# Transposing the normalized attention output: TensorE and a DVE copy, or the DMA crossbar

## The chip, the core and the metric

The kernel runs on one core of a Trainium2 chip. The metric is device time in microseconds for one execution. The core's engines that matter here are TensorE (PE in the profile, its weight loads PEld), VectorE (DVE), ScalarE (ACT), GpSimd (POOL, which here issues the loads) and SyncE (SP, which here does nothing but issue DMAs). Each engine works through its own instructions in order, and semaphores hold an instruction back until what it needs is there.

## The reference: attention with a relative bias, then a mixture of adapters

The first half is attention over 8 batches, 8 heads, 576 positions and a head size of 64, with a bias that depends on the distance of two positions; the second half adds to each of the 4608 tokens a gated sum of the two best of 8 low-rank adapters.

```python
scores = scale * np.matmul(q, k.transpose(0, 1, 3, 2)) + bias
attn = exp(scores - max) ; attn = attn / sum(attn)
x = np.matmul(attn, v)            # then rows = tokens (4608), columns = 8 heads x 64 = 512
logits = x @ w_gate               # 512 -> 8
topk = the two largest; w = softmax over those two
out = x + sum_k w_k * ((x @ A[e_k]) @ B[e_k])     # A: 512 -> 16, B: 16 -> 512
```

The products `x @ w_gate` and `x @ A` sum over the 512 columns of x. TensorE sums over partitions, and attention leaves x with tokens on the partitions. So x has to be transposed between the two halves. That transpose is what the change is about.

## The kernel before, in words

The outer loop (L502) runs over 32 pairs of heads, four per batch, and one more turn, `i` = 32, that finishes the last pair. In turn `i`, five blocks `g` of 128 keys (the fifth holds the 64 tail keys of both heads) each get score matmuls (`qk`, L258 to L268), an exponential on ACT (L275) and a multiplication by the bias factor on DVE (`band`, L282 to L293). In the same turn PE also transposes k and q of the next pair (`transposes`, L247, copied out by DVE in L250) and multiplies the probabilities of the previous pair with v (`pv_main`, L304 and L310, at g = 1; `pv_rest`, L324 to L336, at g = 2). DVE divides those products by their sums and writes them into x as bf16 (`norm_main`, L347 and L348, token blocks 0 to 2; `norm_rest`, L356 to L360, block 3 and the 64 tail tokens).

When the last pair of a batch has been normalized (turn `i` a multiple of 4, g = 2), the second half for that batch is put in a queue of pieces (`pieces`, L477). At g = 0, 3 and 4 of each turn one piece is taken from it (L528, L529). The pieces are, in order: `m_x` half 0, `m_x` half 1, for odd batches `m_xtail` (the 128 tail tokens of two batches, by a selecting matmul), `m_gate` (logits, top two, weights; the matmul is L399, its copy out L404), the same for the tail, `m_z` (L431, L436), `m_zT` (L447, L449), four `m_out` (matmul L455, sum L457, store issued by SP in L460) and for odd batches `m_outt` (L465 to L475, two stores). What is left after the last turn is run in a row.

Odd batches have 14 pieces and a batch has 12 places, so two pieces are left over for the next batch: batches 2, 4 and 6 begin with the last `m_out` and the `m_outt` of the batch before. Seen from the place where x is complete (turn `i`, g = 2), the first matmul of the gate is therefore issued in turn `i`+1 at g = 0 for batch 0, at g = 3 for batches 1, 3 and 5, at g = 4 for batches 2, 4 and 6, and for batch 7 in the closing row, directly after `m_xtail`.

`m_x` works on half of a batch's 512 main tokens: eight transposes of 128x128 on PE into a PSUM tile `xps` (L375), and one DVE copy of 128x1024 into `xT` (L377). `xps` comes from the pool `acc`, which has two buffers for everything but the scores: the transposed k and q, the attention products, and all tiles of the second half. `xT` has two buffers as well.

Loads are issued by POOL, which also converts f32 to bf16 on the way; the loads of v for the batch after next and its tails are held back until `pv_rest` of the last pair has freed their buffer, that is, until about the time when x is complete (L69, L96, L105). There is no planner: the order on each engine is the order of the calls.

Of the kernel before, what the change touches and what calls it, by code (L numbers as in the profile page):

```python
# [11 lines left out]
BF16 = mybir.dt.bfloat16  # L12
# [15 lines left out]
def kernel(  # L28
# [11 lines left out]
    nc = tc.nc  # L40
# [22 lines left out]
    acp = ctx.enter_context(tc.tile_pool(name="acc_ps", bufs=2, space=PSUM))  # L63
# [49 lines left out]
    ident = cp.tile([128, 128], BF16, tag="ident")  # L113
# [40 lines left out]
    for h0, h1 in ((0, 2), (2, H)):  # L154
        nc.sync.dma_start(
            out=Mr[:, h0:h1, :],
            in_=bass.AP(tensor=gt.tensor, offset=gt.offset + h0 * 512,
                        ap=[[1, 128], [512, h1 - h0], [1, MW]]))
        if h0 == 0:
            for e in range(2):  # L160
                nc.sync.dma_start(
                    out=MHr[e * 64:(e + 1) * 64],
                    in_=bass.AP(tensor=gt.tensor, offset=gt.offset + e * 512 + 192,
                                ap=[[1, 64], [1024, HP], [1, 192]]))
# [54 lines left out]
    for i in range(2):  # L219
        t = cp.tile([128, HP, 3, 128], BF16, name=f"tlT{i}", tag=f"tlT{i}")  # L220
# [74 lines left out]
    def pv_main(i):  # L295
        b, hp = divmod(i, HP)
        vn, vt = vns[b % 2], vts[b % 2]
        acc = acp.tile([128, 3, 2, D1], FP32, name="pvA", tag="acc")
        first = True
        for g in range(5):  # L300
            p = probs[(i, g)]
            for qb in range(3):
                if g == 4:
                    nc.tensor.matmul(acc[:, qb], lhsT=p[:, qb * 128:(qb + 1) * 128],  # L304
                                     rhs=vt[:, hp, :], start=False, stop=True,
                                     skip_group_check=True)
                    continue
                for h in range(2):
                    o = h * 512 + qb * 128
                    nc.tensor.matmul(acc[:, qb, h, :], lhsT=p[:, o:o + 128],  # L310
                                     rhs=vn[:, g, 2 * hp + h, :], start=first,
                                     stop=False, skip_group_check=True)
                    first = False
        return acc

    def pv_rest(i):
        b, hp = divmod(i, HP)
        vn, vt = vns[b % 2], vts[b % 2]
        acc = acp.tile([128, 2, 2, D1], FP32, name="pvB", tag="acc")
        first = True  # L320
        for g in range(5):
            p = probs[(i, g)]
            if g == 4:
                nc.tensor.matmul(acc[:, 0], lhsT=p[:, 384:512],  # L324
                                 rhs=vt[:, hp, :], start=False, stop=True,
                                 skip_group_check=True)
                nc.tensor.matmul(acc[:, 1], lhsT=p[:, 512:640], rhs=vt[:, hp, :],
                                 start=False, stop=True, skip_group_check=True)
                continue
            for h in range(2):  # L330
                o = h * 512 + 384
                nc.tensor.matmul(acc[:, 0, h, :], lhsT=p[:, o:o + 128],
                                 rhs=vn[:, g, 2 * hp + h, :], start=first,
                                 stop=False, skip_group_check=True)
                first = False
            nc.tensor.matmul(acc[:, 1], lhsT=p[:, 1024:1152],  # L336
                             rhs=vn[:, g, 2 * hp:2 * hp + 2, :], start=False,
                             stop=False, skip_group_check=True)
        return acc
# [27 lines left out]
    def m_x(b, half):  # L367
        x = xs[b]
        if half == 0:
            st[(b, "xT")] = xp.tile([128, 4, S4], BF16, name="xT", tag="xT")  # L370
        xT = st[(b, "xT")]
        ps = acp.tile([128, 4, 256], BF16, name="xps", tag="acc")
        for t2 in range(2):
            for c in range(4):
                nc.tensor.transpose(ps[:, c, t2 * 128:(t2 + 1) * 128],  # L375
                                    x[:, 2 * half + t2, 2 * c:2 * c + 2, :], ident)
        nc.vector.tensor_copy(xT[:, :, half * 256:(half + 1) * 256], ps)  # L377

    def m_xtail(b):

# [96 lines left out]
    def pieces(b):  # L477
        km, kt = (b, "m"), (b, "t")
        l = [lambda: m_x(b, 0), lambda: m_x(b, 1)]
        tl = b % 2 == 1  # L480
        if tl:
            l.append(lambda: m_xtail(b))
        l.append(lambda: m_gate(km, st[(b, "xT")], 4))
        if tl:
            l.append(lambda: m_gate(kt, st[(b, "xT", "t")], 1))
        l.append(lambda: m_z(km, st[(b, "xT")], 4))
        if tl:
            l.append(lambda: m_z(kt, st[(b, "xT", "t")], 1))
        l.append(lambda: m_zT(km, 4))
        if tl:  # L490
            l.append(lambda: m_zT(kt, 1))
        for t in range(4):
            l.append(lambda t=t: m_out(b, t))
        if tl:
            l.append(lambda: m_outt(b))
        return l
# [5 lines left out]
    for i in range(NPAIR + 1):  # L502
# [10 lines left out]
        for g in range(5):  # L513
# [6 lines left out]
            if g == 1 and i > 0:  # L520
                acc = pv_main(i - 1)
                norm_main(i - 1, acc)
            if g == 2 and i > 0:
                acc = pv_rest(i - 1)
# [41 lines left out]
```

The softmax here doesn't subtract the row's maximum and nothing guards it: scores larger than these inputs give would overflow.

## Time and profile before

| what | value |
|---|---|
| time, median of two runs | 258.7 us (258.33 and 259.07) |
| span of the profiled execution, first to last instruction | 257.7 us |
| own time of the profiled execution | not given apart; the two runs stand 0.6 and 1.4 us above the span, 1.0 by their median |
| DVE busy | 205.9 us, 641 instructions |
| PE busy | 189.7 us, 2576 matmuls |
| ACT busy | 165.4 us, 174 instructions |
| L375, transposes of x on PE | 128, 9.8 us in all |
| L377, copies of them on DVE | 16, 10.9 us in all, 682 ns each |
| L399, gate matmuls | 128 for the main tokens, 166 ns each |
| loads, queue of POOL | 14.16 MB, 112768 packets, 89.6% of the time of 16 DMA engines |
| DMAs of SP and others, hardware queue | 10.97 MB, 14.6% |

Busy times of different engines overlap, and so do the packets of different DMA queues, so the shares do not add up to one. The batches follow each other at about 26 to 27 us; the last pair is normalized near 241 us, and the rest is the closing row for batch 7.

### The profile page before, as it was taken

Reading aid. Unit: us, or ns where it says so; the run is one execution under the profiler, and the core shown is the slowest. Engines: PE = TensorE matmul, PEld = TensorE weight load, DVE = VectorE, ACT = ScalarE, POOL = GpSimd, SP = SyncE. Lnnn points to the kernel's source line nnn. Section 1 sums busy time; section 2 is a strip of 40 time slices with the busy share of each in tenths; the row PEclk is TensorE's granted clock in tenths of the full one; section 3 lists DMA queues with packets and bytes.
Section 4 is the critical chain, followed back from the end, with each engine's and each line's share of the span. In section 5 each row is a group of like instructions: output and inputs, shape, how many; then the busy total and the mean of one; then the engine's idle time right before and its main releaser. Section 6 shows DMA issues by size and latency. Waiting matters only on the chain.

```text
span 257.7 us, 6522 instructions
## 1 busy us (share of the span) xinstructions
PE 189.7 (74%) x2576; PEld 120.1 (47%) x2576; DVE 205.9 (80%) x641; ACT 165.4 (64%) x174; POOL 117.3 (46%) x155
## 2 busy tenths in 40 slices
PE   0020698797878868897799778987898788888852
PEld 0010255465545655456356554564465544664710
DVE  3200678999898888999979898989998889989972
ACT  2000469897769767886688677867796678868100
POOL 8997999745733591185508560549052000000000
PEclk9999999999999999999889999999999999999965
DMA  4999999969893999399939992799969003202205
GB/s 27 141 154 153 94 131 114 137 42 99 85 201 54 105 84 84 122 146 85 163 95 107 58 142 34 133 166 101 147 109 69 0 3 123 84 3 83 85 21 183
DMA packets 124759, 25.56 MB, mean 99 GB/s; under 512 B 118960, under 2 KB 119992, under 8 KB 124728
## 3 DMA queue, kind: packets, MB, share of 16 engines
q0 software_dynamic: 112768, 14.16, 89.6%
q1 hardware_dynamic: 11960, 10.97, 14.6%
q8 instruction: 20, 0.33, 0.5%
q14 instruction: 11, 0.09, 0.1%
HBM read 29.84 MB, written 9.45 MB: 152 GB/s over the span
## 4 chain that ended last, share of the span: by engine, by line
DVE 50%; PE 26%; ACT 7%; POOL 6%; issue 5%; DMA 3%; ACTq 0%; POOLq 0%; DVEq 0%
PE pvA L310 11%; DVE x L348 6%; PE sc L262 5%; DVE x L360 3%; DVE kqT L250 3%; DMA vn_86<-in_v_dram 3%; DVE o L457 3%; DVE xT L377 3%; PE pvA L304 2%; PE kqps L247 2%; DVE rcA L347 2%; POOL qn L69 2%; DVE rmB L358 2%; PE sc L258 1%; PE dl L455 1%
## 5 line engine op out<-in xcount | busy, mean ns | idle before, releaser
L262 PE MATMUL sc<-kqT 64*128 64x512 bf16 x256 | 51.8, 402 | 0.0
L69 POOL DMA_DIRECT2D kn<-in_k_dram x36 | 31.2, 896 | 19.1 <-PE kqps L247 18.2
L69 POOL DMA_DIRECT2D qn<-in_q_dram x36 | 31.0, 906 | 1.6 <-DMA vn_86<-in_v_dram 1.5
L258 PE MATMUL sc<-tlT_184,kqT 128*128 128x128 bf16 x64 | 14.5, 226 | 18.3 <-DVE kqT L250 13.0
L69 POOL DMA_DIRECT2D vn_87<-in_v_dram x16 | 14.0, 894 | 28.4 <-PE pvB L336 28.4
L69 POOL DMA_DIRECT2D vn_86<-in_v_dram x16 | 14.0, 896 | 27.7 <-PE pvB L336 27.6
L262 PEld LDWEIGHTS <-kqT 64*128 64x128 bf16 x256 | 12.4, 93 | 26.5 <-issue 17.4
L250 DVE COPY kqT<-kqps 128x1024 bf16<-128x1024 bf16 x32 | 21.8, 683 | 3.5 <-PE kqps L247 3.4
L457 DVE TENSOR_TENSOR o<-dl,x 128x512 f32<-128x512 f32 x32 | 21.8, 683 | 1.6 <-DMA out_dram<-o 0.8
L258 PEld LDWEIGHTS <-kqT 128*128 128x128 bf16 x128 | 12.8, 100 | 17.7 <-DVE kqT L250 13.2
L348 DVE TENSOR_TENSOR x<-pvA,rcA 128x384 bf16<-128x384 f32 x32 | 17.8, 557 | 1.1
L455 PE MATMUL dl<-Bb,zT 128*128 128x512 bf16 x32 | 13.3, 421 | 6.8 <-DVE zT L449 2.8
L275 ACT ACTIVATE p_227<-sc 128x1152 bf16<-128x1152 f32 x1 | 1.1, 1131 | 23.4 <-PE sc L262 23.4
L239 DVE COPY tlT_184<-tps 64x512 bf16<-64x512 bf16 x8 | 3.4, 419 | 15.4 <-POOL tlT_184 L221 15.3
L258 PE MATMUL sc<-tlT_186,kqT 128*128 128x128 bf16 x64 | 14.2, 222 | 1.7 <-ACT p_571 L275 0.7
L360 DVE TENSOR_TENSOR x<-pvB,rmB 128x256 bf16<-128x256 f32 x32 | 13.6, 424 | 1.1
L347 DVE RECIPROCAL rcA<-pvA 128x6 f32<-128x6 f32 x32 | 6.2, 195 | 10.1 <-PE pvA L304 9.9
L247 PE MATMUL kqps<-ident,kn 128*128 128x128 bf16 x128 | 13.3, 229 | 1.0 <-DVE o L457 0.6
L412 ACT ACTIVATE ex<-df 128x32 f32<-128x32 f32 (+1 forms) x12 | 2.7, 222 | 17.0 <-DVE df L409 17.0
L234 PE MATMUL tps<-ident,tl 128*128 128x128 bf16 x32 | 3.4, 232 | 13.3 <-DMA tl<-in_q_dram 13.3
L247 PE MATMUL kqps<-ident,qn 128*128 128x128 bf16 x128 | 13.1, 228 | 0.0
L247 PEld LDWEIGHTS <-kn 128*128 128x128 bf16 x128 | 8.2, 101 | 7.5 <-issue 6.8
(1431 smaller groups left out, 655.4 us busy)
## 6 DMA issues: line engine op xcount, KB each, us to landing
out_dram<-o SPq DMA_DIRECT2D x32, 256.0 KB, 2.1
kn<-in_k_dram POOLq DMA_DIRECT2D x28, 128.0 KB, 4.1
qn<-in_q_dram POOLq DMA_DIRECT2D x28, 128.0 KB, 4.7
vn_86<-in_v_dram POOLq DMA_DIRECT2D x16, 128.0 KB, 5.1
vn_87<-in_v_dram POOLq DMA_DIRECT2D x16, 128.0 KB, 4.4
out_dram<-o SPq DMA_DIRECT2D x8, 128.0 KB, 4.6
Mr<-g_d SPq DMA_DIRECT2D x1, 576.0 KB, 6.6
tl<-in_k_dram POOLq DMA_DIRECT2D x8, 64.0 KB, 4.0
```

The lines of the kernel that those rows point to most:

```text
L69: nc.gpsimd.dma_start(out=o, in_=src[b, h0:h1, j * 128:(j + 1) * 128, :] .rearrange("h p d -> p h d"))
L247: nc.tensor.transpose(ps[:, w, j * 128:(j + 1) * 128], n[:, j, 2 * hp:2 * hp + 2, :], ident)
L250: nc.vector.tensor_copy(t, ps)
L258: nc.tensor.matmul(sc[:, 1024:1152], lhsT=t[:, 0, g * 128:(g + 1) * 128], rhs=tt[:, hp, 1, :], start=True, stop=True)
L262: nc.tensor.matmul(sc[:, h * 512:(h + 1) * 512], lhsT=t[s, 0, g * 128:(g + 1) * 128], rhs=t[s, 1, :], start=True, stop=True)
L310: nc.tensor.matmul(acc[:, qb, h, :], lhsT=p[:, o:o + 128], rhs=vn[:, g, 2 * hp + h, :], start=first, stop=False, skip_group_check=True)
L347: nc.vector.reciprocal(rc, acc[:, :, :, D])
L348: nc.vector.tensor_tensor(x[:, 0:3, 2 * hp:2 * hp + 2, :], acc[:, :, :, :D], rc.unsqueeze(3).to_broadcast((128, 3, 2, D)), op=ALU.mult)
L360: nc.vector.tensor_tensor(x[:, 3:5, 2 * hp:2 * hp + 2, :], acc[:, :, :, :D], rm.unsqueeze(3).to_broadcast((128, 2, 2, D)), op=ALU.mult)
L377: nc.vector.tensor_copy(xT[:, :, half * 256:(half + 1) * 256], ps)
L455: nc.tensor.matmul(ps, lhsT=zT[:, t, :], rhs=Bb, start=True, stop=True)
L457: nc.vector.tensor_tensor(o, ps, xs[b][:, t].rearrange("p h d -> p (h d)"), op=ALU.add)
```

## The change

The two transposes of `m_x` through PE and PSUM are replaced by two transposing DMAs, issued by SP, from x to xT directly. Each handles one token block: 128 partitions (tokens) by 512 bf16 columns, 128 KB, and writes four blocks of 128x128 side by side. A batch has four of them; in all 32 transposing DMAs stand for 128 PE transposes and 16 DVE copies, and 16 tiles of the pool `acc` are no longer taken. Everything else has the same text.

```diff
         xT = st[(b, "xT")]
-        ps = acp.tile([128, 4, 256], BF16, name="xps", tag="acc")
         for t2 in range(2):
-            for c in range(4):
-                nc.tensor.transpose(ps[:, c, t2 * 128:(t2 + 1) * 128],
-                                    x[:, 2 * half + t2, 2 * c:2 * c + 2, :], ident)
-        nc.vector.tensor_copy(xT[:, :, half * 256:(half + 1) * 256], ps)
+            t = 2 * half + t2
+            nc.sync.dma_start_transpose(out=xT[:, :, t * 128:(t + 1) * 128],
+                                        in_=x[:, t].rearrange("p h d -> p (h d)"))
```

In the changed kernel's order of instructions, the four transposes of a batch stand together on SP, between the stores of the batch before and the stores of their own. Each waits for x (blocks 0 to 2 for `norm_main`, block 3 for `norm_rest`), for the last reader of its `xT` buffer, and for a DMA eight places before it in SP's queue, whose semaphore it takes over. The gate's 16 matmuls go by token block, and the weight load of each block waits for its transpose's semaphore: the first four for block 0, and so on.

## The prediction

> **What bounds the kernel now.** First I read the busy times and the shares of the chain that ended last.
>
> ```profile
> PE 189.7 (74%) x2576; PEld 120.1 (47%) x2576; DVE 205.9 (80%) x641; ACT 165.4 (64%) x174; POOL 117.3 (46%) x155
> ...
> DVE 50%; PE 26%; ACT 7%; POOL 6%; issue 5%; DMA 3%; ACTq 0%; POOLq 0%; DVEq 0%
> ```
>
> DVE is the busiest engine and half of the chain, PE a quarter. DMA has 3% of the chain, all near the start, so the loads do not bound the kernel: in POOL's timeline each batch's loads wait 3 to 11 us for free buffers. Next I looked in the chain, in order of time, for the two lines that the change removes.
>
> ```profile
> 56.99 0.60 DVE xT L377
> ...
> 58.05 0.60 DVE xT L377
> ...
> 112.11 0.61 PE xps L375 x8
> ...
> 116.62 0.60 DVE xT L377
> ```
>
> Batch 0 has both copies on the chain; batch 2 has one copy and one group of eight PE transposes. Batches 1, 3 and 5 are like batch 0, batches 4 and 6 like batch 2. Batch 7 has one copy and one group (0.63).
>
> **Removed.** On the chain stand 2 + 3x1 + 3x2 + 1 = 12 copies at 0.60 = 7.2 us, and 3x0.61 + 0.63 = 2.5 us of PE: 9.7 us. The other four copies overlap what PE does, and cost nothing now. So at most about 9.7 us go away: 1.2 us ahead of the gate in each of batches 0 to 6, 1.3 in batch 7. ACT leaves room for it: a turn lasts 6 to 8 us, and ACT needs about 5.2 of them (four exponentials at some 1.13, one at 0.70).
>
> **Added: a wait on the DMAs.** In PE's order the gate's matmuls stand ahead of the next block's scores, so while they wait, ACT gets no scores and the other matmuls queue behind; on DVE the copy L404 waits for the gate and holds the bias multiplications and normalizations behind it. The question is when four transposes have landed, measured from the moment SP may start them. Call that D. The cover in each batch is the distance to L404, in DVE's and SP's timeline:
>
> ```profile
> 54.75 0.56 DVE L348 TENSOR_TENSOR x<-pvA,rcA 128x384 bf16<-128x384 f32 x1
> ...
> 59.38 0.18 DVE L404 COPY lg<-lp 128x32 f32<-128x32 f32 x1
> ...
> 80.79 0.56 DVE L348 TENSOR_TENSOR x<-pvA,rcA 128x384 bf16<-128x384 f32 x1
> ...
> 89.17 0.18 DVE L404 COPY lg<-lp 128x32 f32<-128x32 f32 x1
> ...
> 112.09 1.18 SPq L475 DMA_DIRECT2D out_dram<-o  x2
> ...
> 117.67 0.19 DVE L404 COPY lg<-lp 128x32 f32<-128x32 f32 x1
> ...
> 240.09 0.56 DVE L348 TENSOR_TENSOR x<-pvA,rcA 128x384 bf16<-128x384 f32 x1
> ...
> 243.46 0.19 DVE L404 COPY lg<-lp 128x32 f32<-128x32 f32 x1
> ```
>
> Blocks 0 to 2 may go when L348 ends, block 3 one microsecond later, which the issue of the first three covers. After the last landing four gate matmuls remain, about 0.3 us (16 took 0.56). In the new order L404 would come 1.2 us earlier (1.3 in batch 7).
> - Batch 0: start 55.31, L404 due at 58.18. Loss D - 2.6.
> - Batches 1, 3, 5: start 81.35, due 87.97. Loss D - 6.3.
> - Batches 2, 4, 6: the stores of the batch before occupy SP until 113.27, and the transposes are queued behind them; due 116.47. Loss D - 2.9.
> - Batch 7: start 240.65, due 242.16; here nothing but the tail's transpose lies beside. Loss D - 1.2.
>
> A negative loss counts as zero. After such a stall DVE has no store of work, so I take no recovery. The other side of the sum: the stores of a batch are queued behind its own transposes, but come a turn or more later, so they cost nothing.
>
> **D itself** is in no row of this trace; there is no transposing DMA. I bound it as three issues plus one landing (the landing is counted from its issue).
>
> ```profile
> L475 SPq DMA_DIRECT2D out_dram<-o x8: 472/560/592, 112.1 to 254.2; - x8
> ...
> L69 POOL DMA_DIRECT2D kn<-in_k_dram x36: 738/900/1038, 1.2 to 176.3; - x36
> ...
> L206 SPq DMA_DIRECT2D A_f<-in_moe_A_dram x4: 540/1414/2413, 9.2 to 14.5; - x4
> ...
> out_dram<-o SPq DMA_DIRECT2D x32, 256.0 KB, 2.1
> kn<-in_k_dram POOLq DMA_DIRECT2D x28, 128.0 KB, 4.1
> ...
> A_f<-in_moe_A_dram SPq DMA_DIRECT2D x4, 64.0 KB, 6.7
> ```
>
> Low: plain stores of SP, 3x0.56 + 2.1 = 3.8 us. High: the load of A in 64-byte runs, 3x1.41 + 6.7 = 10.9 us. Middle: the load of k, as many bytes as a transpose, in 256-byte pieces (1024 of them), 3x0.90 + 4.1 = 6.8 us. I take 6.8: a transpose has 512 source runs of 256 bytes and must scatter them, so it is nearer to that load than to rows written whole. Moreover, the transposes of batches 0 to 5 start together with POOL's loads of v, freed by the same last matmul, and beside them SP's 128 KB stores landed in 4.6 to 5.1 us against 2.3 at the quiet end.
>
> VectorE: DVE Perf Modes, section on the three transpose paths, in the Trainium skill, gives 390 ns for a 128x128 transpose on TensorE and 1309 ns on the DMA crossbar, and advises TensorE if PSUM will do. This trace shows 219 ns for one on PE, 0.61 us for eight in a row. If the crossbar's 1309 ns were a pace, 16 of them make D about 20.9 us, an estimate from that page, and the sum about 385 us; as a latency, with blocks overlapping, it would lie with my low end.
>
> **The clock.** After a stretch in which PE has little to do, the trace shows the granted clock fall:
>
> ```profile
> 246.00:249.00 3.00, 0.98 (x6) 0.58 (x7) 2.01 (x8) 0.16 (x1) 0.00 (x0) 0.59 0.00 0
> 249.00:252.00 3.00, 2.45 (x6) 0.58 (x5) 1.98 (x3) 0.00 (x0) 0.00 (x0) 0.50 0.36 136
> ```
>
> The columns are the stretch and its length, PE, PEld, DVE, ACT and POOL busy (with counts), then the clock, DMA share and GB/s. The clock is 0.59 and 0.50, where it was 1.00 before; and L455's matmul takes up to 634 ns, 390 in the median. Stalls of 4 us in batches 0, 2, 4 and 6 could do the same. Bounds for each: nothing, if the clock holds; and 1.9 us, if 3 us of PE work run at 634/390. I take 1.0, the middle, since nothing here shows how fast it comes back: 4 us.
>
> TensorE: Matmul & The Clock Gate, section "Why this matters for your kernels", in the Trainium skill, says to avoid idle gaps above about 3 us because the clock drops; by that rule the stalls of 4 us would pay and those of 1 us would not.
>
> **The sum.** With D = 6.8: 4.2 + 3x0.5 + 3x3.9 + 5.6 = 23.0 us of stalls, less 9.7, plus 4 for the clock: +17.3 on 257.7, a span of 275.0. The median of the runs lies 1.0 above the span: 276.0 us, 6.7% slower. The other ends: D = 3.8 gives 1.2 + 0 + 2.7 + 2.6 = 6.5, less 9.7: 255.5 us. D = 10.9 gives 8.3 + 13.8 + 24.0 + 9.7 = 55.8, less 9.7, plus up to 7.6 for the clock: 304.8 to 312 us. The two sides balance at D = 4.4 without the clock.
>
> **The rivals.**
> 1. *The wait replaces the copies* (forecast, D from 5.5 to 8.5): by the same losses 264 us without a clock term to 290 with 4 us of it, likeliest 276. For it: covers of 1.2 to 2.9 us in five of eight batches, against the 3.8 us that even plain stores need. Against: no row shows a transposing DMA. Chance 0.47.
> 2. *Cheap transposes*, D from 3.5 to 5.5, near SP's plain stores: 254 to 264 us, within 2%. For it: hardware-queue packets of 2 KB move beside the loads in 84 to 96 ns, so the engines are not full, and SP is idle between stores. Chance 0.21.
> 3. *Faster*: the four land before L404 misses them. One mechanism, at the wait of L399: at SP's shortest issue in this trace (0.40, L117) and 2.1 to land, D = 3.3, the stalls are 0.7 + 1.2 + 2.1 = 4.0, and 257.7 - 5.7 + 1.0 = 253.0 us; with D under 1.2 all 9.7 remain, 249.0. It decides from D = 3.4 downwards. For it: x is complete a whole turn ahead of the gate in batches 1 to 6. Against: SP is still storing in 2, 4 and 6. Chance 0.08.
> 4. *A transposing DMA occupies the queue far longer than a load*, D above 8.5: 290 us and up, 305 to 312 at 10.9, and 8 us more for each further microsecond of D, since all eight batches then stall. Every single transpose makes 4096 runs of 32 bytes on the destination side, if 16 rows go at a time as the instruction's tile size (16 rows, 128 columns) says. Chance 0.24, of which above 310 us 0.11.
> That the transposes stay on PE is excluded: the changed order has no L375 left, and 32 transposing DMAs on SP.
>
> **How the numbers follow.** Predicted 276 us. The range 255 to 310 leaves out the faster cases (0.08) and the far end of the fourth (0.11). A measurement of this kernel tells about 2%, 5.2 us, from no change. Faster by over 2%: 0.08. Within: 0.21. Slower: 0.71.
>
> **What the changed profile would show.** Right: L399's weight loads wait for DMA xT, about 4 us in batches 0, 2, 4 and 6, under 1 in 1, 3 and 5, over 5 in 7; DVE's L404 idle for as long; a clock below 1.00 after it; DVE busy 10.9 us less, PE 9.8 less. The issue row of the transposes gives D: below 0.6 us each and landing in 2, rival 2 or 3 has it; above 1.4, rival 4. I am wrong if the gate's wait shows under 1.5 us in batches 0 and 2, or if the transposes slow the loads until PE waits for k or q.

## The result and the profile after

The changed kernel takes 299.75 us (median of two runs, 299.38 and 300.12) against 258.7: the ratio is 1.158, 95% interval 1.151 to 1.164. The profiled execution's span is 298.3 us against 257.7, 40.6 us more. The forecast was slower by 17 us; the sign was right, and the loss is more than twice as large. Where a kernel below was run four times, its time is the median of its fast runs; one run of one control was slow (269.51 us) and is left out.

The page of the changed kernel: busy times, the shares of the chain that ended last by engine and by line, and two of its costliest groups (busy and mean, then idle time before and what ended it).

```profile
PE 198.6 (67%) x2444; PEld 125.2 (42%) x2448; DVE 198.6 (67%) x625; ACT 165.5 (55%) x174; POOL 117.3 (39%) x155
...
PE 31%; DMA 19%; DVE 16%; issue 11%; POOL 9%; ACT 8%; SPq 5%; POOLq 0%; ACTq 0%; DVEq 0%
DMA xT<-x 14%; PE pvA L310 8%; PE sc L262 8%; ACT p L275 7%; SPq L374 5%; DMA vn<-in_v_dram 5%; PE kqps L247 4%; POOL qn L69 3%; DVE p L289 3%; POOL kn L69 3%; PE zp L429 3%; PE sc L258 2%; DVE o L455 2%; DVE x L348 2%; PE pvA L304 1%
...
L397 PE MATMUL lp<-Wb,xT 128*128 128x8 bf16 x128 | 8.4, 172 | 42.2 <-DMA xT<-x 42.2
...
L402 DVE COPY lg<-lp 128x32 f32<-128x32 f32 (+1 forms) x12 | 2.2, 181 | 42.4 <-PE lp L397 42.4
```

DVE is busy 7.3 us less, and its share fell from 80% to 67%: it waits. The chain, half DVE before, now has 14% in the transposes' DMAs and 5% in their issue on SP (L374). L397 and L402 are the old L399 and L404: the gate's matmuls waited 42.2 us for the transposes, and the copy of their logits, with all of DVE behind it, 42.4 us. Neither waited for a DMA before:

```profile
L399 PE MATMUL lp<-Wb,xT 128*128 128x8 bf16 x128 | 4.9, 167 | 2.7 <-DVE xT L377 2.7
...
L404 DVE COPY lg<-lp 128x32 f32<-128x32 f32 (+1 forms) x12 | 2.1, 176 | 0.0
```

The two points that the prediction measured from, in the changed kernel. SP's timeline has the start of each batch's four transposes, POOL's the start of the loads of v, DVE's the arrival of the logits with the idle time before it. In each view, batches 0, 1 and 2 are shown, and for SP and DVE batch 7, beside which nothing is loaded.

```profile
54.40 5.38 SPq L374 DMA_TRANSPOSE xT<-x  x4
...
90.60 5.30 SPq L374 DMA_TRANSPOSE xT<-x  x4
...
128.19 5.86 SPq L374 DMA_TRANSPOSE xT<-x  x4
...
276.64 5.83 SPq L374 DMA_TRANSPOSE xT<-x  x4
```

```profile
54.45 3.50 POOL L69 DMA_DIRECT2D vn<-in_v_dram  x4 [4.94 <-PE pvB L336]
...
90.65 3.50 POOL L69 DMA_DIRECT2D vn<-in_v_dram  x4 [9.61 <-PE pvB L336]
...
123.62 3.50 POOL L69 DMA_DIRECT2D vn<-in_v_dram  x4 [10.52 <-PE pvB L336]
```

```profile
65.82 0.19 DVE L402 COPY lg<-lp 128x32 f32<-128x32 f32 x1 [7.72 <-PE lp L397]
...
103.96 0.19 DVE L402 COPY lg<-lp 128x32 f32<-128x32 f32 x1 [6.04 <-PE lp L397]
...
136.35 0.19 DVE L402 COPY lg<-lp 128x32 f32<-128x32 f32 x1 [5.08 <-PE lp L397]
...
284.05 0.19 DVE L402 COPY lg<-lp 128x32 f32<-128x32 f32 x1 [5.67 <-PE lp L397]
```

From these and the like rows of the other batches comes this table. D runs from SP's first transpose to the start of the gate's last four matmuls. "x to logits" is from the end of L348 to the start of the logits' copy; "then to next x" is from there to the end of the next batch's L348.

| batch | D after | x to logits, before | after | then to next x, before | after |
|---|---|---|---|---|---|
| 0 | 11.1 | 4.07 | 11.44 | 21.97 | 24.76 |
| 1 | 13.1 | 7.82 | 13.38 | 19.55 | 19.57 |
| 2 | 7.9 | 8.95 | 12.82 | 18.67 | 17.95 |
| 3 | 11.8 | 7.82 | 12.12 | 19.55 | 19.57 |
| 4 | 8.3 | 8.95 | 13.24 | 17.30 | 18.76 |
| 5 | 10.5 | 7.82 | 10.92 | 19.55 | 20.14 |
| 6 | 6.5 | 8.96 | 11.77 | 14.36 | 15.76 |
| 7 | 7.1 | 2.81 | 7.47 | | |

The first pair of columns adds up to +36.0 us, the second to +5.6; the start up to batch 0 is 0.9 shorter, the closing row after the last logits as long as before (14.2). That is the 40.6 us: nearly all of it lies between x and the logits, where the prediction had looked, but D is 6.5 to 13.1 and not 6.8. The two batches at the end, beside which no load runs, have the shortest. In batches 0, 1, 3 and 5 the transposes start within 0.1 us of the loads of v; in 2 and 4 they start 4.5 us after them, behind the stores on SP.

The issue of a transpose on SP, and its time to land, in the changed kernel:

```profile
L374 SPq DMA_TRANSPOSE xT<-x x32: 1196/1276/1899, 54.4 to 281.3; - x32
...
DMA to landing us min/median/max: 2.4/4.8/9.0
```

One takes 1.28 us to issue, against 0.56 for a plain store on the same queue. Its landing lies between 2.4 and 9.0 us. Asked by stretch, the median of the four landings is 6.4, 8.2, 5.9, 5.3, 4.3 and 6.5 us in batches 0 to 5, and 2.5 in batches 6 and 7.

### The profile page after: what moved, and what is told of

It is laid out like the page before. It is cut to its first block, busy times and chain, and to the rows that moved or that the text cites. A ratio compares the mean times of both kernels' runs of the same rounds, so it can differ in the third digit from the quotient of the medians.

```text
span 298.3 us, 6299 instructions
## 1 busy us (share of the span) xinstructions
PE 198.6 (67%) x2444; PEld 125.2 (42%) x2448; DVE 198.6 (67%) x625; ACT 165.5 (55%) x174; POOL 117.3 (39%) x155
## 3 DMA queue, kind: packets, MB, share of 16 engines
q1 hardware_dynamic: 29368, 15.17, 22.9%
## 4 chain that ended last, share of the span: by engine, by line
PE 31%; DMA 19%; DVE 16%; issue 11%; POOL 9%; ACT 8%; SPq 5%; POOLq 0%; ACTq 0%; DVEq 0%
DMA xT<-x 14%; PE pvA L310 8%; PE sc L262 8%; ACT p L275 7%; SPq L374 5%; DMA vn<-in_v_dram 5%; PE kqps L247 4%; POOL qn L69 3%; DVE p L289 3%; POOL kn L69 3%; PE zp L429 3%; PE sc L258 2%; DVE o L455 2%; DVE x L348 2%; PE pvA L304 1%
## 5 line engine op out<-in xcount | busy, mean ns | idle before, releaser
L275 ACT ACTIVATE p<-sc 128x1152 bf16<-128x1152 f32 (+1 forms) x160 | 161.8, 1043 | 60.5 <-PE sc L262 58.6
L289 DVE TENSOR_TENSOR p<-p,M 128x512 bf16<-128x512 bf16 (+1 forms) x128 | 62.4, 489 | 2.6 <-ACT p L275 1.9
L69 POOL DMA_DIRECT2D vn<-in_v_dram x32 | 28.1, 894 | 55.6 <-PE pvB L336 55.5
L258 PE MATMUL sc<-tlT,kqT 128*128 128x128 bf16 x128 | 29.5, 230 | 20.9 <-DVE kqT L250 12.4
L397 PE MATMUL lp<-Wb,xT 128*128 128x8 bf16 x128 | 8.4, 172 | 42.2 <-DMA xT<-x 42.2
L310 PEld LDWEIGHTS <-p 128*128 128x128 bf16 x768 | 29.2, 103 | 10.4 <-issue 8.5
L310 PE MATMUL pvA<-vn,p 128*128 128x65 bf16 x768 | 32.0, 201 | 2.0 <-DVE tlT L240 0.6
L402 DVE COPY lg<-lp 128x32 f32<-128x32 f32 (+1 forms) x12 | 2.2, 181 | 42.4 <-PE lp L397 42.4
L397 PEld LDWEIGHTS <-xT 128*128 128x128 bf16 x128 | 5.7, 104 | 46.2 <-DMA xT<-x 45.5
L250 DVE COPY kqT<-kqps 128x1024 bf16<-128x1024 bf16 x32 | 21.9, 686 | 4.7 <-PE kqps L247 4.7
L258 PEld LDWEIGHTS <-kqT 128*128 128x128 bf16 x128 | 13.1, 102 | 17.6 <-DVE kqT L250 12.7
L332 PE MATMUL pvB<-vn,p 128*128 128x65 bf16 x256 | 19.3, 197 | 0.0
L336 PE MATMUL pvB<-vn,p 128*128 128x130 bf16 x128 | 18.7, 220 | 0.0
L348 DVE TENSOR_TENSOR x<-pvA,rcA 128x384 bf16<-128x384 f32 x32 | 17.8, 557 | 1.1
L332 PEld LDWEIGHTS <-p 128*128 128x128 bf16 x256 | 15.4, 98 | 7.4 <-issue 7.2
```

Source lines behind the costliest of these rows:

```text
L69: nc.gpsimd.dma_start(out=o, in_=src[b, h0:h1, j * 128:(j + 1) * 128, :] .rearrange("h p d -> p h d"))
L250: nc.vector.tensor_copy(t, ps)
L258: nc.tensor.matmul(sc[:, 1024:1152], lhsT=t[:, 0, g * 128:(g + 1) * 128], rhs=tt[:, hp, 1, :], start=True, stop=True)
L275: nc.scalar.activation(p, sc[:, :n], ACT.Exp, scale=scale)
L289: nc.vector.tensor_tensor(pm[:, :, q0:q1], pm[:, :, q0:q1], Mh[:, :, x0:x0 + q1 - q0], op=ALU.mult)
L310: nc.tensor.matmul(acc[:, qb, h, :], lhsT=p[:, o:o + 128], rhs=vn[:, g, 2 * hp + h, :], start=first, stop=False, skip_group_check=True)
```

## The experiments

**The theory** after this reading: a transpose costs 1.28 us of SP's queue, and POOL's loads of v and tails, which the same last matmul sets free, lengthen its landing. **The rival:** transposes in the middle of the kernel are late by themselves, say because engines use the same memory. A second question is what the removed work was worth.

### Without the loads beside the transposes

```diff
-            if hp == 1 and b + 1 < B:
+            if hp == 1 and b + 1 < 2:
                 load_v(b + 1)
...
-                load_tails(b + 1)
+                if b + 1 < 2:
+                    load_tails(b + 1)
```

The tail tile of later batches is that of batch 0 or 1. Expected:

> The changed kernel, but from batch 2 on v and the 64 tail tokens are not loaded (the buffers keep batch 0 and 1, so these batches compute with old data). Theory: what made D (from SP's first transpose of a batch to the last landing) 8 to 13 us in batches 0 to 5 instead of 6.4 to 7.1 in batches 6 and 7 is POOL's loads of v and tails, which start at the same moment. Then D is about 6.4 in every batch, the copy L402 waits about 4 us in batches 0, 2, 4, 6, under 0.5 in 1, 3, 5 and 5.7 in 7, and the time is about 274 us. Rival: a transposing DMA lands late in the middle of the kernel by itself (engines reading and writing the same memory): D stays at 8 to 13 and the time at 295 to 300 us.

The same two edits made to the kernel before are the control:

> The kernel before with the same loads left out, as the control: the loads are not on its chain after the start, so 257 to 260 us. If it falls by more than 2%, part of what the run beside it gains is not the transposes'.

Measured: 281.62 us and 258.28 us, beside 259.79 for the kernel before on the same chip, in one run each. The transposes in the run without the loads:

```profile
L375 SPq DMA_TRANSPOSE xT<-x x32: 1196/1252/2193, 55.7 to 262.8; - x32
...
DMA to landing us min/median/max: 2.4/2.5/4.2
```

They land in 2.5 us in the median, and D is 6.4 to 7.4 us in the batches that still wait. The logits' copy waits 3.08 us in batch 0, 0.28, 0.39 and nothing in 1, 3, 5, 3.66 to 4.19 in 2, 4, 6, and 5.91 in 7. The rival falls: the same transposes at the same places land early when the loads are gone, and the control gains only 1.5 us from their absence, no more than single runs of one kernel differ (258.16 to 259.84 us). The waits came out close to what was expected. The total is 8 us above the expectation; the removed work, which paid back some 5 us less than I had booked (below), can account for the larger part.

### With the loads held back

```diff
-            if hp == 1 and b + 1 < B:
+            if hp == (1 if b == 0 else 2) and b + 1 < B:
+                if b > 0:
+                    nc.gpsimd.tensor_copy(hold, st[(b - 1, "lg")][:, 0, 0:1])
                 load_v(b + 1)
```

The one-column copy makes POOL, and with it the loads behind, wait until the logits of the batch are out. Expected:

> The changed kernel with all loads, but POOL issues those of v for the batch after next (and the tails, k and q behind them in its queue) only once the gate's logits of the batch have been copied out: a one-column copy of lg on POOL is put before them. Theory: the same as without these loads, D about 6.4 and about 274 us, as POOL has 5 to 13 us of waiting per batch to give. Rival 1: the transposes are late by themselves, 295 to 300 us. Rival 2: the loads, begun 9 to 13 us later, come late for the next batch and PE waits for v, k or q instead: 280 us or more with waits on DMA vn, kn or qn of several us.

Measured: 279.82 us in one run, 20 us under the changed kernel, with every byte loaded. POOL waits for the logits now (in this kernel's chain of waits, the first line; the others are the gate's):

```profile
POOL hold L514 <- DVE lg L402: 90.3, 6, 17.9
...
PE lp L397 <- DMA xT<-x: 22.3, 21, 2.5
DVE lg L402 <- PE lp L397: 21.9, 7, 5.4
```

90.3 us of POOL's waiting cost next to nothing, as PE's waits for loads after the start come to 0.7 us in all, and the gate's wait on DVE halves from 42.4 to 21.9 us. So of the 40 us of loss about half came from the collision with the loads. The other half remains with D at 6.4 to 7.6 us, as in the run without loads, against covers that are mostly shorter.

### The three batches for which the prediction had forecast next to no stall

Batches 1, 3 and 5 alone by DMA, the others on PE as before, once with the loads as they were and once with them held (`m_xpe` is the old code on PE and DVE):

```diff
-        l = [lambda: m_x(b, 0), lambda: m_x(b, 1)]
         tl = b % 2 == 1
+        f = m_x if tl and b < B - 1 else m_xpe
+        l = [lambda: f(b, 0), lambda: f(b, 1)]
```

> Batches 1, 3 and 5 transposed by DMA, the other five on PE as before. The prediction's step for these three (D = 6.8 against a cover of 6.3, so 0.5 us of stall each, less 1.2 us of removed work each) gives a gain of 2.1 us: 256.6 us. The changed kernel's trace (13.0, 11.7 and 10.5 us from start to last landing, beside the loads) gives stalls of 3 to 5 us each net: 270 to 274 us.

> The same three batches by DMA, with the loads of v held back until the gate's logits are out, in all batches. If the loads alone make the loss of these three, D is 6 to 6.5, the wait at the gate under 0.7 us each, and the time 256 to 260 us. If not, 268 us or more.

Measured, one run each, beside 258.99 us: 273.94 and 259.51 us. The waits of the two kernels, first with the loads free and then held:

```profile
DVE lg L414 <- PE lp L409: 15.1, 3, 5.5
PE lp L409 <- DMA xT<-x: 15.1, 10, 2.2
```

```profile
PE lp L409 <- DMA xT<-x: 1.6, 4, 0.9
DVE lg L414 <- PE lp L409: 1.1, 2, 0.6
```

Three batches lose 15 us by themselves, and the copy of their logits waits 15.1 us. With the loads held they are as fast as on PE: three sets of transposes with a counted cover of 6.3 us cost nothing that can be measured (their logits wait 1.1 us in all). They gain nothing either, where 2 us had been forecast; one run cannot tell such a gain from the 1.7 us by which runs of the kernel before differ.

### One transposing DMA per batch

```diff
-            st[(b, "xT")] = xp.tile([128, 4, S4], BF16, name="xT", tag="xT")
+            st[(b, "xT")] = xp.tile([128, 4, 4, 128], BF16, name="xT", tag="xT")
+            return
...
+        nc.sync.dma_start_transpose(out=xT.rearrange("p t c q -> p (t c) q"),
+                                    in_=x[:, 0:4].rearrange("p t h d -> p (t h d)"))
```

> The changed kernel with one transposing DMA of 128x2048 per batch in place of four of 128x512 (xT laid out by token block for it). If SP's 1.28 us per transpose is paid per block of 16 rows by 128 columns (32 of them in 128x512, 128 here), one issue takes 4.5 to 5.1 us, D changes little, and as the one DMA also waits for block 3 and the gate waits for all of it, the time is 298 to 306 us. If it is paid per instruction, the issue takes about 1.3 us, D falls by 3 us or more, and the time is 275 to 285 us.

Measured: 305.77 us in one run. SP's timeline in this kernel, a batch beside loads and the two without:

```profile
160.07 4.24 SPq L373 DMA_TRANSPOSE xT<-x  x1
...
263.31 1.95 SPq L373 DMA_TRANSPOSE xT<-x  x1
...
284.37 2.93 SPq L373 DMA_TRANSPOSE xT<-x  x1
```

Neither account of the issue held. Four times the bytes take 1.95 and 2.93 us where nothing is loaded, so the cost is neither per block nor per instruction alone, and 4.0 to 4.6 us beside the loads, where this longer issue grows. That of the small transposes does not: its median is 1.25 us in batch 6 and 1.27 to 1.32 in batches 0 to 5 of the changed kernel. The time lies in the range of the first account, but for another reason: beside the loads the DMA waits for the last token block, and over the eight batches it lands 9.6 us after its issue in the median, so the logits wait longer than with four DMAs. In batch 7, without loads, it landed in 4.7 us; the logits' copy waited 4.38 us instead of 5.67 there, and 2.32 instead of 4.04 in batch 6.

### What the removed work was worth

The kernel before, with transposes and copies of x left out and nothing in their place (xT keeps a constant, so the gates are computed from it):

```diff
+    xTs = [cp.tile([128, 4, S4], BF16, name=f"xT{n}", tag=f"xT{n}") for n in range(2)]
...
     def m_x(b, half):
...
+        st[(b, "xT")] = xTs[b % 2]
```

> The kernel before with the transposes of x and their copies left out and nothing in their place (xT keeps a constant, so the gates are wrong): the worth of the removed work by itself. The prediction's chain count says 9.7 us, so 249 us. Rival: ACT or PE takes over as soon as DVE has less to do, and only about half is to be had, 253 to 256 us.

Measured: 254.55 us against 258.99, ratio 0.980 (0.974 to 0.986), four runs against seven; the fastest of the four took 251.81. So leaving the transposes out, at no cost at all, brings some 5 us at these places; the chain had said 9.7. The profiled execution shows where the rest went. From x to the logits the batches take 7.1 us less in all: 1.3 each in batches 2, 4 and 6 and 1.1 in batch 7, about as counted, but only 0.4 to 0.6 in batches 0, 1, 3 and 5, where both copies stood on the chain. In these four the chain now runs through two exponentials of ACT in a row (2.26 us), and ACT begins the list by line; by engine it had 7% of the chain before and has 14% now:

```profile
by line: ACT p L275 12.8%; PE pvA L310 11.4%; DVE p L289 8.1%; PE sc L262 8.0%; issue 4.5%; PE kqps L247 3.6%; DVE x L348 3.5%; DMA vn<-in_v_dram 3.2%; DVE kqT L250 3.1%; DVE o L452 2.7%; PE pvA L304 2.3%; PE sc L258 2.2%; DVE tlT L239 2.2%
```

Between the logits and the next x, 2.1 us are lost again, and these go with the granted clock. Batches 0, 3 and 4 take 1.3, 0.8 and 1.3 us more there, and the clock is 0.57 from 73 to 77 us, 0.66 from 144 to 149 and 0.66 from 178 to 183. Batch 2 takes 1.4 us less: there it is the kernel before that has a low clock, 0.51 from 127 to 130 us. Elsewhere between 38 us and the closing row it is 1.00 in both, and batches 1, 5 and 6 take the same time as before. Why the clock falls at these places was not tested. The last 0.7 us lie ahead of batch 0's x, where nothing had been removed.

### All of it covered

Transposes of batches 0 to 6 issued as soon as x is complete and thus ahead of the stores left over, loads held until they have landed, empty places (`wait`) in the queue of pieces so that the gate is the fifth piece, batch 7 on PE.

```diff
+        if b == B - 1:
+            l = [lambda: m_xpe(b, 0), lambda: m_xpe(b, 1)]
+        else:
+            m_x(b, 0)
+            m_x(b, 1)
+            l = []
...
+        if b < B - 1:
+            l += [wait] * (4 if b == 0 else 3 if tl else 1)
         l.append(lambda: m_gate(km, st[(b, "xT")], 4))
...
+                if b > 0:
+                    nc.gpsimd.tensor_copy(hold, st[(b - 1, "xT")][:, 0, 0:S4:128])
                 load_v(b + 1)
```

> All that was found put together: batches 0 to 6 by DMA, their transposes issued as soon as x is complete (ahead of the stores left over from the batch before), the loads of v held until they have landed, the gate taken from the queue as the fifth piece instead of the first to third, and batch 7, which has no cover, on PE. If a wait of D = 6.4 us and its cover are the whole story, no gate waits and the removed work shows: 249 to 253 us. If the transposes cost something beside the wait, it stays at 256 us or more.

The same without the two lines that hold the loads:

> The covered version without holding the loads of v: transposes issued when x is complete, the gate as the fifth piece, batch 7 on PE. The cover is then some 8 to 9 us in every batch. If the loads lengthen D to 10 to 13 us whenever both start together, now in batches 2 and 4 as well, the gate waits 2 to 4 us in batches 0 to 5 and the time is 264 to 275 us. If a cover of 8 us is enough, 255 to 258 us.

And with PE and DVE transposing in all batches, at the places where the DMAs were issued:

> Control for the covered version: the same places for the gate and the same held loads, but x transposed on PE and copied by DVE in all batches, at the place where the DMAs were issued. If the covered version's gain of 2.3 us is that of work taken off PE and DVE, this is at 258 to 262 us. If it comes from the new places of the pieces, this is at 256 to 257 us too.

| kernel | time, us | before, same chip | ratio, 95% interval |
|---|---|---|---|
| covered, loads held | 256.65 | 258.99 | 0.989 (0.984 to 0.995) |
| covered, loads free | 282.72 | 258.59 | 1.090 (1.083 to 1.097) |
| same places, on PE | 264.59 | 258.59 | 1.023 (1.017 to 1.029) |

The covered kernel is 1.1% faster than the kernel before: a small gain, but its interval leaves out 1. It is less than expected, and 256 us or more was to mean that the transposes cost something beside the wait. But the lower range had counted on 9.7 us of removed work, and the kernel that transposes nothing takes 254.55 us itself. Batch 7 on PE (1.1 us from x to the logits) and 1.3 us of remaining waits at the gate would make up the 2.1 us between the two, so no further cost of the transposes is needed to explain it. The line that holds the loads is worth 26 us here. Without it the gate waits 22.7 us although it has 8 to 9 us of cover:

```profile
DVE lg L414 <- PE lp L409: 22.7, 6, 5.2
```

and batches 2 and 4, which in the changed kernel started 4.5 us after the loads, behind the stores (D of 7.9 and 8.3), now start together with the loads as well and take 11 us from x to the logits instead of 8.8. The control on PE, slower than the kernel before, shows that the new places did not make the gain. It is not a pure one: on PE the transposes, all issued at one place, wait for DVE's normalization (5.8 us on L375's weight loads, 2.2 in the kernel before), which costs time that the DMAs don't.

## Why the prediction was wrong in size, point by point

**What bounds the kernel; where the change acts: right.** Nearly all of the loss appears at L399 and L404 (L397 and L402 after), through the wait that was named, with covers about as counted. In the two batches without loads the forecast wait is the measured one: 3.9 us against 4.04 in batch 6, 5.6 against 5.67 in batch 7. Put the measured D of the table into the prediction's own losses and they give 8.5 + 6.8 + 5.0 + 5.5 + 5.4 + 4.2 + 3.6 + 5.9 = 44.9 us of stalls, less 9.7, plus 4 for the clock: a span of 296.9, where 298.3 was measured. Part of that closeness is chance: the logits' copy in fact waited 42.4 us, the removed work was worth less than 9.7, and the stretches behind the logits grew by more than 4.

**D = 6.8 us for every batch: the step that failed.** The term was sized from the row of the load of k, 3x0.90 + 4.1. In its place the runs show two numbers. Without loads, the last landing of four transposes comes 6.4 to 7.6 us after SP's start (issues of about 1.28 us, landing in 2.5): the total was near, though both parts differ from the row, so that is partly luck. Beside the loads of v it comes 8 to 13 us after. The prediction named this collision, with the stores' 4.6 to 5.1 us against 2.3, and then used it to choose one D within its bounds instead of giving the batches that start with the loads a D of their own. Above all it charged batches 1, 3 and 5 half a microsecond of stall each, since their cover of 6.3 is the longest; they have the longest cover and started exactly with the loads. Measured alone, they lose 15 us against a forecast gain of 2.

**The removed 9.7 us: too high.** Taken out by itself, the work is worth 4.4 us by the medians, 5.2 by the ratio. Adding up the pieces of the chain on two lines assumes that nothing else is late next; the prediction said that ACT leaves room, from 5.2 us of exponentials in a turn of 6 to 8. Averaged over a turn it does, but not at these places: in batches 0, 1, 3 and 5 of the run without transposes, ACT's exponentials stand on the chain ahead of the logits, and 0.4 to 0.6 us go away where 1.2 had been counted. That makes 2.6 us of the difference; 2.1 go with the clock and 0.7 with the start.

**The clock: about right.** It did fall after the stalls. In the changed kernel around batch 0's stall, with the clock as the number after POOL's busy time:

```profile
61.00:65.00 4.00, 0.54 (x8) 0.37 (x8) 0.00 (x0) 0.00 (x0) 0.00 (x0) 0.50 2.05 130
65.00:69.00 4.00, 3.49 (x41) 2.31 (x42) 2.67 (x15) 1.30 (x3) 0.00 (x0) 0.50 0.02 4
69.00:73.00 4.00, 3.48 (x40) 2.42 (x38) 2.87 (x9) 2.92 (x3) 0.00 (x0) 0.76 0.00 0
73.00:77.00 4.00, 3.81 (x63) 2.63 (x61) 3.40 (x9) 2.98 (x3) 2.98 (x4) 1.00 0.54 46
```

PE is busy again from 65.5 us on, and is at half clock until 69 and at full clock by 73. The stretch from the logits to the next x is 2.8 us longer there, and 5.6 us in all batches together; 4 had been charged. PE as a whole is busy 8.9 us longer, without its 128 transposes of x. That this is all the clock's doing was not shown. Batch 2's stretch is shorter than before, but there the kernel before had a granted clock of 0.51 from 127 to 130 us, and took 18.67 us for the stretch against 17.30 in batch 4, where the clock was 1.00. The Trainium skill advises against PE-idle gaps above about 3 us, since the clock then drops (TensorE: Matmul & The Clock Gate, "Why this matters for your kernels"). These traces agree only loosely: in batch 0's stall the clock was down although the longest gap was 2.77 us, with groups of four gate matmuls (0.27 us) between the gaps; and ahead of the drop at 127 us PE had been busy for 3.37 of 5 us, with no gap above 0.8 us.

**The Trainium skill's 1309 ns per 128x128 block** (VectorE: DVE Perf Modes, "The three transpose paths") is not a pace here: a 128x512 block, four times that, is issued every 1.28 us and, undisturbed, lands 2.4 to 2.6 us after its issue. What bears more on the loss stands on another page of the Trainium skill, which the prediction did not weigh: DMAs from SP, ACT and POOL run on the same 16 engines and interleave (DMA: Bandwidth & Descriptors, "Issuing engines are not separate DMA queues"). Running beside the loads cost this here: medians of a batch's landings of 4.3 to 8.2 us with them, of 2.5 without. That the interleaving is how it comes about was not tested.

**The rivals.** Cheap transposes and the faster case are out. The measured time lies where the fourth rival had it, 290 us and up. That a transposing DMA takes longer than a load was put at D above 8.5, and by D that is what batches 0, 1, 3 and 5 show; its reason, many short runs on the destination side, is not: without the loads a transpose lands as fast as a 128 KB store in the quiet end of the kernel before (2.3 us). The prediction read the 3% of DMA in the chain as a sign that the loads do not bound the kernel. That was true as long as no DMA of that moment was on the path.

**The signs.** Waits at the gate of about 4 us in batches 0, 2, 4 and 6, under 1 in 1, 3 and 5 and over 5 in 7 had been named; the logits waited 7.72, 5.08, 5.50 and 4.04 us, then 6.04, 4.77 and 3.56, and 5.67. So batches 0, 1, 3 and 5 are furthest off. The issue of 1.28 us lies between the two thresholds named, 0.6 and 1.4, and decided nothing. PE never waited as much as 1 us for k or q.

## What to carry to other kernels

The transposes, put on a chain that had no DMA there, were held up by the transfers that the same event set free. So ask which other DMAs start at that moment, and size its landing from rows measured beside them, place by place, not once for all. A DMA in place of engine work needs an issue pace times the number of pieces plus a landing as cover, and, as here, a one-column copy that delays prefetches with slack can be worth more than the change itself. And take a chain's share of a line as the ceiling of what its removal brings; a run with the work left out says how much of it is there.

## What the runs showed of the hardware that was not expected

- A transposing DMA of 128x512 bf16 occupies SP for 1.28 us (median of 32; plain 128 KB stores 0.56), one of 128x2048 for 1.95 and 2.93 us without loads beside it and for 4.0 to 4.6 us beside them. Undisturbed, the small one lands 2.4 to 2.6 us after its issue; right behind a 256 KB store one took 3.7.
- Each adds 544 packets to the hardware queue: 29368 of them after, 11960 before, for 32 transposes.
- The granted clock fell to half for some 3 us in the kernel before (0.51 from 127 to 130 us), with PE busy for two thirds of the 5 us ahead of it.
- Beside loads that convert to bf16, of 128 KB each, a transpose lands up to 9.0 us after its issue. How the queues share the engines, and why batch 1 was worst, was not settled.
